# Moving the second pair of heads of the second batch behind the third feed-forward step

## The chip, the cores and the metric

The kernel runs on one core of one Trainium2 chip. The metric is the device time of one execution in microseconds; of the kernel before, three runs gave 924.9, 925.16 and 926.29 us, a median of 925.16 us. The engines are TensorE (PE in the profile, with PEld for its weight loads), VectorE (DVE), ScalarE (ACT), GpSimd (POOL) and SyncE (SP), which issues all data transfers here.

## The reference

Two parts follow each other. The first is attention over 8 batches of 8 heads, 576 tokens, 64 values a head; heads 0 to 3 see a window of the last 32 keys, heads 4 to 7 a window of 32 keys at a distance of 4. The second is a feed-forward layer over the 4608 tokens.

```
scores = scale * np.matmul(q, k.transpose(0, 1, 3, 2))
...
scores = np.where(masks[None, :, :, :], scores, -1000000000.0)
scores = scores - np.max(scores, axis=-1, keepdims=True)
attn = np.exp(scores)
attn = attn / (np.sum(attn, axis=-1, keepdims=True) + 1e-09)
return np.matmul(attn, v).astype(np.float32)
...
h = x @ w_in
g = np.where(pos, h, np.where(neg, 0.0, (h + beta) ** 2 / (4.0 * beta)))
return (g @ w_out).astype(np.float32)
```

w_in is 512 x 2048, w_out 2048 x 512. x is the attention's output with the heads of a token side by side.

## The kernel before, in words

Tokens are cut into 9 tiles of 512, the hidden dimension into 16 blocks of 128. A step is one tile and one block, so there are 144 steps; the first 16 are those of tile 0. Layer 1 of a step (L398) makes 12 products of 128 x 128 by 128 x 512 into one PSUM bank named h: each operand is held as a rounded part and a remainder, and three of the four cross terms are taken. Then DVE clips (L412), ACT squares (L415), DVE takes the maximum back into the bank (L417), ACT rounds it to gh (L418) and DVE makes the remainder gl (L421). Layer 2 (L434) runs two steps behind and adds 12 products into four banks named acc. There are two banks h, so layer 1 of step s waits for gl of step s-2.

Attention runs beside it. For heads 8 to 15 (the second batch) it goes in pairs (n, n+1), and each pair has five parts on TensorE: scores of four of six query tiles (L202), scores of the other two, transposes of n, transposes of n+1 (L325), and values (L360). DVE reduces each score tile with its mask (L176), softmax follows on POOL, ACT and DVE (L250, L284 to L286, L291 to L293), the transposes are copied out of PSUM by ACT and DVE (L328), and the values are copied out as a rounded part xh (ACT, L344) and a remainder xl (DVE, L345), in up to three pieces where a head's tokens cross a tile's border. Scores, transposes and values of these pairs share two PSUM banks (tag "att"): whatever comes next in one of them waits until the last reader of what stood there is done.

The weights arrive as 64-bit floats. For each of the 32 blocks ACT makes two passes over the words (L116, L120), DVE joins them (L121), ACT rounds (L126), POOL makes the remainder (L127). These blocks are prepared during the first 16 steps: from step 1 on, each step brings the layer-2 block of its own number and the layer-1 block three further on, behind the rounding of two steps earlier (L603 to L607). A buffer m, three deep, links L116 to the L127 of three blocks earlier.

The order on TensorE and on SP is that of the code (manual schedule). On DVE, ACT and POOL the compiler's scheduler fixes the order when the program is built, by its own estimate of times and by the priorities in the code; on the chip each of them then works in that order. A table (L479) gives the places of the pairs' parts: place 2s is between layer 1 of step s and layer 2 of step s-2, place 2s+1 is behind that layer 2. In the numbers of a tile's name, t10 is the transposes of head 10, o8 the values of heads 8 and 9, s12 the scores of head 12. At step 2 TensorE makes constant products that nothing reads (L610), after which layer 1 of step 2 follows.

Of the kernel before, what the change touches and what calls it, by code (L numbers as in the profile page):

```python
# [30 lines left out]
B, H, S, D = 8, 8, 576, 64  # L31
# [14 lines left out]
def body(ctx, tc, q, k, q2, k2, v, mask, eye, w_in, w_out, out):  # L46
# [23 lines left out]
    def load_pair(n):  # L70

        if 0 < n < H:
            qr, kr = borrow(f"qr{n}")[:, :S], borrow(f"kr{n}")[:, :KPAD]
        else:
            tags = ("qs", "kk") if n % 4 else ("qr", "kr")
            qr = pool.tile([128, S], F32, tag=tags[0], name=f"qr{n}")
            kr = pool.tile([128, KPAD + 32], F32, tag=tags[1], name=f"kr{n}")[:, :KPAD]
        nc.sync.dma_start(out=qr, in_=q[n // 2])
        nc.sync.dma_start(out=kr, in_=k[n // 2])
        for j in range(2):  # L80
            r = slice(64 * j, 64 * j + 64)
            heads[n + j] = dict(qs=qr[r], ks=kr[r])

    def load(n):
        qr = pool.tile([128, S], F32, tag="qr", name=f"qr{n}")
        kr = pool.tile([128, KPAD + 32], F32, tag="kr", name=f"kr{n}")[:, :KPAD]
        nc.sync.dma_start(out=qr, in_=q2[n - native])
        nc.sync.dma_start(out=kr, in_=k2[n - native])
        heads[n] = dict(qr=qr, kr=kr)
# [39 lines left out]
    def split(n):  # L129
        hd = heads[n]  # L130
        qs = pool.tile([128, S], F32R, tag="qs", name=f"qs{n}")
        kk = pool.tile([128, 2, KPAD], F32R, tag="kk", name=f"kk{n}")
        nc.scalar.copy(out=qs, in_=hd["qr"])
        nc.scalar.copy(out=kk[:, 0], in_=hd["kr"])  # L134
        nc.vector.tensor_tensor(
            out=qs[64:128], in0=hd["qr"][64:128], in1=qs[64:128].bitcast(F32), op=ALU.subtract
        )
        nc.gpsimd.tensor_tensor(out=kk[:, 1], in0=hd["kr"], in1=kk[:, 0].bitcast(F32), op=ALU.subtract)  # L138
        hd.update(qs=qs, ks=kk)
# [15 lines left out]
    def spin(times, bank):  # L155

        half = half_t.broadcast_to([128, 128])
        for _ in range(times):
            PE.matmul(out=bank[:, :128], lhsT=half, rhs=half, start=True, stop=True)  # L159
# [117 lines left out]
    def softmax(n):  # L277
        c, st = heads[n]["c"], heads[n]["st"]
        if n in (8, 9, 10, 12, 14):
            whole(n)  # L280
        else:
            for t in range(NQ):
                exp(n, t)
        nc.scalar.activation(out=st[:, 1], in_=st[:, 1], func=AF.Copy, bias=EPS)  # L284
        nc.vector.reciprocal(out=st[:, 2], in_=st[:, 1])  # L285
        nc.gpsimd.tensor_tensor(out=c, in0=c, in1=spread(st[:, 2]), op=ALU.mult)  # L286
# [43 lines left out]
    last = {}  # L330
    xt = {}

    def xtile(t):
        if t not in xt:
            xt[t] = (
                pool.tile([128, NC, TOK], F32R, tag="xh", name=f"xh{t}", bufs=3),
                pool.tile([128, NC, TOK], F32R, tag="xl", name=f"xl{t}", bufs=3),
            )
        return xt[t]
# [51 lines left out]
    def layer1(t, f, cs=range(NC), bank=("h", 2)):  # L391
        xh, xl = xtile(t)
        if cs[0] == 0 and (t, f) not in hps:
            hps[t, f] = ps.tile([128, TOK], F32, tag=bank[0], name=f"h{t}_{f}", bufs=bank[1])
        hp = hps[t, f]
        terms = [(w, x, c) for c in cs for w, x in ((0, xh), (1, xh), (0, xl))]
        for i, (w, x, c) in enumerate(terms):
            PE.matmul(  # L398
                out=hp,
                lhsT=wi[f][:, w, 128 * c : 128 * c + 128],  # L400
                rhs=x[:, c],
                start=c == 0 and i == 0,
                stop=c == NC - 1 and i == len(terms) - 1,
            )
        if cs[-1] < NC - 1:
            return
        del hps[t, f]
        y = pool.tile([128, TOK], F32, tag="y", name=f"y{t}_{f}")
        gh = pool.tile([128, TOK], F32R, tag="gh", name=f"gh{t}_{f}", bufs=2)
        gl = pool.tile([128, TOK], F32R, tag="gl", name=f"gl{t}_{f}", bufs=2)  # L410
        with tc.high_priority(offset=60):
            nc.vector.tensor_scalar(  # L412
                out=y, in0=hp, scalar1=-1.0, scalar2=1.0, op0=ALU.max, op1=ALU.min
            )
            nc.scalar.activation(out=y, in_=y, func=AF.Square, bias=half_t, scale=0.5)  # L415

            activated = nc.vector.tensor_tensor(out=hp, in0=hp, in1=y, op=ALU.max)  # L417
            copied = nc.scalar.copy(out=gh, in_=hp)  # L418
            if t == 0:
                last["g", f] = copied, activated  # L420
            nc.vector.tensor_tensor(out=gl, in0=hp, in1=gh.bitcast(F32), op=ALU.subtract)  # L421
        gs[t, f] = gh, gl

    acc = {}
# [28 lines left out]
    def place(u, *ops):  # L453
        slots.setdefault(u, []).extend(ops)

    def after_pair(n):
        softmax(n)
        softmax(n + 1)
        if n + 4 < native:
            load_pair(n + 4)  # L460
        elif n + 4 == native:
            load(native)
        else:
            split(native)
            load(native + 1)
# [10 lines left out]
        if n + 2 < native:  # L476
            load_values(n + 2)

    for n, at in ((8, (5, 6, 7)), (10, (1, 2, 8, 9, 10)), (12, (11, 12, 16, 17, 18)), (14, (19, 20, 24, 26, 30))):  # L479
        if n > H:  # L480
            place(at[0], lambda n=n: scores_pair(n, 0, 4))
            place(at[1], lambda n=n: (scores_pair(n, 4, NQ), after_pair(n)))
        turns = (n, n + 1) if n < 14 else (n + 1, n)
        for u, m in zip(at[-3:-1], turns):
            place(u, lambda m=m: transpose_pe(m))
        place(at[-1], lambda n=n: values_native(n))
# [66 lines left out]
    with tc.manual_schedule(engines={mybir.EngineType.PE, mybir.EngineType.SP}):  # L553
        pair(0)
        pair(2)
        pair(4)
        pair(6)
        hps[0, 0] = ps.tile([128, TOK], F32, tag="h", name="h0_0", bufs=2)
        early_transposes(0)
        load_values(8)  # L560
        fetch(1, w_out, "wo")
        fetch(4, w_in, "wi")
        load_pair(10)
        fetch(2, w_out, "wo")
        fetch(5, w_in, "wi")
        fetch(3, w_out, "wo")
        for f in range(6, 9):
            fetch(f, w_in, "wi")
            fetch(f - 2, w_out, "wo")
        early_values(0)  # L570
        early_transposes(2)
        early_values(2)
        first = marks()
        spin(10, hps[0, 0])
        early_transposes(4)
        spin(3, hps[0, 0])
        early_transposes(6)
        behind(first, ("wi", 0), ("wi", 1))
        early_values(4)
        second = marks()  # L580
        layer1(0, 0, range(2))
        early_values(6)
        third = marks()
        behind(second, ("wi", 2))
        layer1(0, 1, range(2))
        scores_pair(H, 0, 4)
        scores_pair(H, 4, NQ)
        for f in range(9, 14):
            fetch(f, w_in, "wi")
            fetch(f - 2, w_out, "wo")  # L590
        with tc.issue_after(third[0].ins), tc.issue_after(third[1].ins):
            after_pair(H)
        behind(third, ("wo", 0), ("wi", 3))
        l2 = 0
        steps = [(t, f) for t in range(NT) for f in range(NF)]
        lag = 2
        for s in range(len(steps) + lag):
            if s == 3:
                for f, src, name in ((12, w_out, "wo"), (13, w_out, "wo"), (14, w_in, "wi")):
                    fetch(f, src, name)  # L600
                for f, src, name in ((14, w_out, "wo"), (15, w_in, "wi"), (15, w_out, "wo")):
                    fetch(f, src, name)
            if 0 < s < NF:  # L603
                todo = [("wo", s)]
                if s + 3 < NF:
                    todo.append(("wi", s + 3))
                behind(last["g", max(s - 2, 0)], *todo)  # L607
            if s == 2:
                acc[0] = ps.tile([128, DM], F32, tag="acc0", name="acc0_0")
                spin(14, acc[0])  # L610
            if s < 2:
                layer1(*steps[s], range(2, NC))
            elif s < len(steps):
                layer1(*steps[s])
            run(2 * s)
            while l2 <= s - lag and l2 < len(steps):
                layer2(*steps[l2])
                l2 += 1
            run(2 * s + 1)
        assert not slots  # L620
# [63 lines left out]
```

## Time and profile before

| | us |
|---|---|
| median of three runs | 925.16 |
| the profiled execution | 924.59 |
| its span, first to last instruction | 922.8 |
| TensorE busy | 905.5 (98%) |
| DVE busy | 671.4 (73%) |
| ACT busy | 494.1 (54%) |
| POOL busy | 240.6 (26%) |
| mean granted TensorE clock | 0.998 |

The profile lists what each engine did in one execution. In a timeline a row is a start, a duration, engine, line and operation, output and inputs; in square brackets stands how long the engine was idle before it and what it was waiting for. Records of one engine overlap a little at their ends, so the distance between two starts is what an instruction takes up. A stretch row gives the busy time of an engine and the granted clock, where 1.00 is 2.4 GHz and 0.50 is 1.2 GHz. All times are microseconds from the start of the span unless marked ns.

### The profile page before, as it was taken

What the parts mean: (1) busy time and instruction counts of PE and PEld (TensorE: products, weight loads), DVE (VectorE), ACT (ScalarE), POOL (GpSimd) and SP (SyncE); (2) the same over time, 40 slices, a digit from 0 to 9 for tenths busy, and PEclk for the clock granted to TensorE, in tenths of its full rate; (3) what the DMA queues carried; (4) which work ended last, traced back from release to release, by engine and by line L of the source; (5) the groups of instructions that cost most, each with busy time, mean ns of one, the idle gap of its engine ahead of it and who ended that gap; (6) DMA issues with size and microseconds to landing.
All of it is one profiled execution on the core that took longest, in us unless ns stands there. A gap on an engine that the chain in (4) does not pass through costs nothing.

```text
span 922.8 us, 14430 instructions
## 1 busy us (share of the span) xinstructions
PE 905.5 (98%) x4886; PEld 743.0 (81%) x4886; DVE 671.4 (73%) x1966; ACT 494.1 (54%) x1352; POOL 240.6 (26%) x155
## 2 busy tenths in 40 slices
PE   7899999999999999999999999999999999999997
PEld 6677788888888888888888888888888888888886
DVE  6787778878888888788887888888888643334333
ACT  6798875555555556555555565555556322222222
POOL 4575453222222222222222222223222000000000
PEclk9999999999999999999999999999999999999999
DMA  9981013221232223112322223222321010001001
GB/s 352 407 309 46 1 27 105 82 64 55 66 116 71 70 71 112 48 61 64 116 71 71 70 64 104 63 71 71 116 71 44 1 46 1 1 1 47 0 1 47
DMA packets 31018, 73.87 MB, mean 80 GB/s; under 512 B 3520, under 2 KB 3808, under 8 KB 30944
## 3 DMA queue, kind: packets, MB, share of 16 engines
q1 hardware_dynamic: 30944, 72.94, 24.2%
q8 instruction: 39, 0.64, 0.3%
q14 instruction: 35, 0.29, 0.1%
HBM read 63.49 MB, written 9.44 MB: 79 GB/s over the span
## 4 chain that ended last, share of the span: by engine, by line
PE 89%; DMA 3%; POOL 2%; issue 2%; ACT 1%; DVE 1%; POOLq 0%; DVEq 0%; SPq 0%
PE acc L434 41%; PE h L398 40%; PE s L225 4%; PE o L360 3%; DMA wi_raw<-w_in 3%; ACT c L250 1%; POOL wi L127 1%; POOL wo L127 1%; POOL c L286 1%; PE s L159 0%; DVE c L293 0%; DVE c L176 0%; PE s L202 0%; PE t L325 0%; DMA out<-out 0%
## 5 line engine op out<-in xcount | busy, mean ns | idle before, releaser
L434 PE MATMUL acc<-wo,gh 128*128 128x512 f32 x1152 | 382.8, 393 | 0.0
L398 PE MATMUL h<-xh,wi 128*128 128x512 f32 x1152 | 356.9, 391 | 1.2 <-DVE gl L421 1.2
L434 PEld LDWEIGHTS acc<-wo,gh 128*128 128x128 f32 x1152 | 216.5, 188 | 47.2
L398 PEld LDWEIGHTS h<-xh,wi 128*128 128x128 f32 x1152 | 209.1, 188 | 39.4 <-DVE gl L421 1.4
L434 PE MATMUL acc<-wo,gl 128*128 128x512 f32 x576 | 225.1, 391 | 0.0
L398 PE MATMUL h<-xl,wi 128*128 128x512 f32 x576 | 224.2, 389 | 0.0
L138 POOL TENSOR_TENSOR kk<-kr,kk 128x608 fp32r<-128x608 f32 x48 | 94.8, 1974 | 413.1 <-ACT kk L134 413.1
L250 ACT ACTIVATE c<-c 96x128 f32<-96x128 f32 x330 | 129.0, 393 | 118.0 <-DVE c L176 118.0
L415 ACT ACTIVATE y<-y,consts 128x512 f32<-128x512 f32 x144 | 104.2, 724 | 117.6 <-DVE y L412 117.4
L418 ACT CAST gh<-h 128x512 fp32r<-128x512 f32 x144 | 84.4, 586 | 123.7 <-PE acc L434 119.9
L412 DVE TENSOR_SCALAR y<-h 128x512 f32<-128x512 f32 x144 | 99.2, 689 | 56.3 <-PE h L398 55.9
L417 DVE TENSOR_TENSOR h<-h,y 128x512 f32<-128x512 f32 x144 | 100.5, 698 | 49.6 <-ACT y L415 48.4
L421 DVE TENSOR_TENSOR gl<-h,gh 128x512 fp32r<-128x512 f32 x144 | 98.8, 686 | 40.9 <-ACT gh L418 40.8
L398 PEld LDWEIGHTS h<-xl,wi 128*128 128x128 f32 x576 | 108.2, 188 | 23.2
L434 PEld LDWEIGHTS acc<-wo,gl 128*128 128x128 f32 x576 | 108.2, 188 | 19.6
L301 DVE STREAM_TRANSPOSE pt<-c 32x192 f32<-32x192 f32 x288 | 106.0, 368 | 6.5 <-POOL c L286 3.1
L244 DVE TENSOR_TENSOR c<-s,msk 96x256 f32<-96x256 f32 (+1 forms) x168 | 61.4, 377 | 35.9 <-PE s L225 34.9
L286 POOL TENSOR_TENSOR c<-c 96x768 f32<-96x768 f32 x56 | 83.4, 1491 | 14.4 <-DVE c L285 14.4
L176 DVE CUSTOM_DVE_ANT_0 c<-s,c 96x128 f32<-96x128 f32 x288 | 70.6, 280 | 1.0
L250 ACT ACTIVATION_READ_ACCUMULATOR c<-c 96x1 f32 x330 | 62.2, 189 | 0.0
L344 ACT CAST xh<-o 128x288 fp32r<-128x288 f32 (+8 forms) x112 | 38.5, 383 | 38.4 <-PE o L360 24.1
L225 PEld LDWEIGHTS s<-kk,qs 128*96 128x96 f32 x288 | 46.3, 161 | 15.6
(57 smaller groups left out, 642.9 us busy)
## 6 DMA issues: line engine op xcount, KB each, us to landing
kr<-k_in SPq DMA_DIRECT2D x56, 304.0 KB, 3.3
qr<-q_in SPq DMA_DIRECT2D x56, 288.0 KB, 2.8
vt<-v_in SPq DMA_DIRECT2D x32, 384.0 KB, 3.9
out<-out SPq DMA_DIRECT2D x36, 256.0 KB, 3.1
wi_raw<-w_in SPq DMA_DIRECT2D x16, 512.0 KB, 9.2
wo_raw<-w_in SPq DMA_DIRECT2D x16, 512.0 KB, 9.6
msk<-mask_in SPq DMA_DIRECT2D x1, 144.0 KB, 3.6
ident<-eye_in SPq DMA_DIRECT2D x1, 36.0 KB, 4.3
```

The costliest lines, as they stand in the source:

```text
L138: nc.gpsimd.tensor_tensor(out=kk[:, 1], in0=hd["kr"], in1=kk[:, 0].bitcast(F32), op=ALU.subtract)
L225: PE.matmul(out=sv[:, t - t0], lhsT=hd["qs"][:, t * QT : (t + 1) * QT], rhs=hd["ks"][:, :, t * QT : t * QT + 128], start=True, stop=True,)
L250: last["act"] = nc.scalar.activation(out=c[:, t], in_=c[:, t], func=AF.Exp, bias=st[:, 0, t : t + 1], scale=-1.0, accum_out=st[:, 1, t : t ...
L286: nc.gpsimd.tensor_tensor(out=c, in0=c, in1=spread(st[:, 2]), op=ALU.mult)
L301: nc.vector.transpose(out=pt[r : r + 32, :, 32 * g : 32 * g + 32], in_=c[32 * g : 32 * g + 32, :, r : r + 32],)
L398: PE.matmul(out=hp, lhsT=wi[f][:, w, 128 * c : 128 * c + 128], rhs=x[:, c], start=c == 0 and i == 0, stop=c == NC - 1 and i == len(terms) - 1,
L412: nc.vector.tensor_scalar(out=y, in0=hp, scalar1=-1.0, scalar2=1.0, op0=ALU.max, op1=ALU.min)
L415: nc.scalar.activation(out=y, in_=y, func=AF.Square, bias=half_t, scale=0.5)
L417: activated = nc.vector.tensor_tensor(out=hp, in0=hp, in1=y, op=ALU.max)
L418: copied = nc.scalar.copy(out=gh, in_=hp)
L421: nc.vector.tensor_tensor(out=gl, in0=hp, in1=gh.bitcast(F32), op=ALU.subtract)
L434: PE.matmul(out=acc[m], lhsT=g[:, r], rhs=wo[f][:, w], start=f == 0 and i == 0, stop=f == NF - 1 and i == len(terms) - 1,)
```

## The change

The first scores of heads 10 and 11 move from place 1 to place 4, the second from place 2 to place 5, the transposes of heads 8 to 11 and the values of heads 8 and 10 one place later each. The softmax of heads 8 and 9 is now issued behind the rounding of step 0 instead of behind the last values of the first batch. The constant products at step 2 are 8, not 14. The pairs 12 and 14 keep their places.

```diff
-    for n, at in ((8, (5, 6, 7)), (10, (1, 2, 8, 9, 10)), (12, (11, 12, 16, 17, 18)), (14, (19, 20, 24, 26, 30))):
+    for n, at in ((8, (6, 7, 8)), (10, (4, 5, 9, 10, 11)), (12, (11, 12, 16, 17, 18)), (14, (19, 20, 24, 26, 30))):
...
-        with tc.issue_after(third[0].ins), tc.issue_after(third[1].ins):
-            after_pair(H)
...
-                spin(14, acc[0])
+                spin(8, acc[0])
             if s < 2:
                 layer1(*steps[s], range(2, NC))
+                if s == 0:
+                    with tc.issue_after(last["g", 0][0].ins):
+                        after_pair(H)
```

On TensorE, at places 10 and 11, the first scores of heads 12 and 13 (s12, s13) stood behind layer 2 of step 3. Before:

```order
L434 MATMUL acc0_3_787<-wo3_817,gh0_3_841 128x512
L434 MATMUL acc0_3_787<-wo3_817,gl0_3_842 128x512
L434 MATMUL acc0_3_787<-wo3_817,gh0_3_841 128x512
L202 MATMUL s12_0_1031<-kr12_618,qr12_617 96x128
L202 MATMUL s13_0_1033<-kr12_618,qr12_617 96x128
```

Now, in the same place:

```order
L360 MATMUL o10_1_1011<-pt1_68,vt10_921 64x96
L360 MATMUL o10_1_1011<-pt0_67,vt10_921 64x96
L360 MATMUL o10_1_1011<-pt1_68,vt10_921 64x96
L202 MATMUL s12_0_1025<-kr12_646,qr12_645 96x128
L202 MATMUL s13_0_1027<-kr12_646,qr12_645 96x128
```

The values of heads 10 and 11 (o10), which stood ahead of that layer 2, now stand directly ahead of the scores; both use the two shared banks.

On ACT, around the copies of those values out of PSUM (xh1 and xh2 from o10) and the work of step 5 (y0_5, gh0_5). Before:

```order
L344 CAST xh1_380<-o10_0_996 128x288
L126 CAST wi9_1061<-wi_m9_1057 128x512
L344 CAST xh1_380<-o10_1_1005 128x160
L415 ACTIVATE y0_5_988<-y0_5_988,consts_66 128x512
L344 CAST xh2_888<-o10_1_1005 128x128
L418 CAST gh0_5_989<-h0_5_975 128x512
L116 ACTIVATE wo_m7_1126<-wo_raw7_587 128x512
L120 ACTIVATE wo_raw7_587<-wo_raw7_587 128x512
```

Now:

```order
L415 ACTIVATE y0_5_972<-y0_5_972,consts_66 128x512
L418 CAST gh0_5_973<-h0_5_959 128x512
L116 ACTIVATE wo_m7_1120<-wo_raw7_587 128x512
L120 ACTIVATE wo_raw7_587<-wo_raw7_587 128x512
L116 ACTIVATE wi_m10_1127<-wi_raw10_589 128x512
L120 ACTIVATE wi_raw10_589<-wi_raw10_589 128x512
L344 CAST xh1_380<-o10_0_1002 128x288
L344 CAST xh1_380<-o10_1_1011 128x160
L126 CAST wo7_1124<-wo_m7_1120 128x512
L126 CAST wi10_1131<-wi_m10_1127 128x512
L344 CAST xh2_917<-o10_1_1011 128x128
```

The copies stood ahead of the rounding of step 5; now the rounding and four passes over the weight blocks wo7 and wi10 stand ahead of them, and two more roundings ahead of the last copy.

On ACT, around the copies of the values of heads 8 and 9 (o8) and the copy of the transposes of head 10 (t10). Before:

```order
L344 CAST xh1_380<-o8_0_870 128x288
L116 ACTIVATE wo_m4_894<-wo_raw4_350 128x512
L418 CAST gh0_3_841<-h0_3_827 128x512
L120 ACTIVATE wo_raw5_354<-wo_raw5_354 128x512
L344 CAST xh1_380<-o8_1_879 128x160
L120 ACTIVATE wi_raw8_356<-wi_raw8_356 128x512
L116 ACTIVATE wi_m7_901<-wi_raw7_352 128x512
L126 CAST wo4_898<-wo_m4_894 128x512
L116 ACTIVATE wo_m5_961<-wo_raw5_354 128x512
L344 CAST xh2_888<-o8_1_879 128x128
L328 COPY pt0_67<-t10_0_929 128x384
```

Now:

```order
L344 CAST xh1_380<-o8_0_899 128x288
L126 CAST wo4_868<-wo_m4_864 128x512
L344 CAST xh1_380<-o8_1_908 128x160
L126 CAST wi7_875<-wi_m7_871 128x512
L116 ACTIVATE wo_m5_945<-wo_raw5_354 128x512
L418 CAST gh0_4_892<-h0_4_878 128x512
L120 ACTIVATE wo_raw6_358<-wo_raw6_358 128x512
L120 ACTIVATE wi_raw9_585<-wi_raw9_585 128x512
L344 CAST xh2_917<-o8_1_908 128x128
L328 COPY pt0_67<-t10_0_935 128x384
```

The copies of o8 stood among the work of step 3 and now stand among that of step 4, the last of them behind that step's rounding.

## Rows read from the trace of the kernel before

**Rows 1.** The page's line of busy times, and two rows of the list of who waited for whom on TensorE (us in total, times, longest us).

```profile
PE 905.5 (98%) x4886; PEld 743.0 (81%) x4886; DVE 671.4 (73%) x1966; ACT 494.1 (54%) x1352; POOL 240.6 (26%) x155
...
PE t L325 <- ACT pt L328: 1.2, 1, 1.2
PE h L398 <- DVE gl L421: 1.2, 1, 1.2
```

**Rows 2.** Stretches of TensorE: from:to, length, busy us (instructions), granted clock, busy share of the transfer engines, GB/s.

```profile
46.00:47.00 1.00, 1.00 (x7) 0.50 1.00 401
...
49.00:50.00 1.00, 1.00 (x11) 0.96 1.02 404
...
98.00:922.00 824.00, 819.92 (x4235) 1.00 0.19 58
```

**Rows 3.** Timeline of TensorE at steps 1 to 3.

```profile
44.62 0.46 PE L202 MATMUL s<-kr,qr 64*96 64x128 f32 x2 [1.62 <-DVE c L176]
45.46 1.01 PE L202 MATMUL s<-kr,qr 64*96 64x128 f32 x6 [0.39 <-DVE c L176]
46.40 4.65 PE L159 MATMUL acc<-consts 128*128 128x128 f32 x28
50.81 0.71 PE L398 MATMUL h<-xh,wi 128*128 128x512 f32 x2
...
58.19 0.73 PE L398 MATMUL h<-xh,wi 128*128 128x512 f32 x2 [1.18 <-DVE gl L421]
```

**Rows 4.** Timeline of TensorE at steps 4 to 8.

```profile
66.28 0.73 PE L398 MATMUL h<-xh,wi 128*128 128x512 f32 x2
...
70.86 0.39 PE L325 MATMUL t<-ident,c 96*128 96x96 f32 x2 [1.23 <-ACT pt L328]
...
74.31 0.70 PE L398 MATMUL h<-xh,wi 128*128 128x512 f32 x2
...
78.56 0.50 PE L434 MATMUL acc<-wo,gh 128*128 128x512 f32 x1
...
81.51 1.12 PE L202 MATMUL s<-kr,qr 64*96 64x128 f32 x16
82.56 0.74 PE L398 MATMUL h<-xh,wi 128*128 128x512 f32 x2
...
97.64 0.71 PE L325 MATMUL t<-ident,c 96*128 96x96 f32 x6 [0.31 <-POOL c L286]
```

**Rows 5.** Timeline of DVE: the clip and the remainder of step 0.

```profile
43.05 0.68 DVE L412 TENSOR_SCALAR y<-h 128x512 f32<-128x512 f32 x1
...
48.23 0.68 DVE L421 TENSOR_TENSOR gl<-h,gh 128x512 fp32r<-128x512 f32 x1
```

**Rows 6.** Groups of instructions between 40 and 100 us: line, engine, operation, shapes, count, then busy us and mean ns of one, then the idle time before them.

```profile
L121 DVE SCALAR_TENSOR_TENSOR wi_m<-wi_m,wi_raw 128x512 uint32<-128x512 uint32 x10 | 9.9, 992 | 1.0 <-ACT wi_m L116 1.0
L121 DVE SCALAR_TENSOR_TENSOR wo_m<-wo_m,wo_raw 128x512 uint32<-128x512 uint32 x9 | 9.9, 1101 | 1.7 <-ACT wo_raw L120 1.5
...
L176 DVE CUSTOM_DVE_ANT_0 c<-s,msk 96x128 f32<-96x128 f32 x34 | 7.6, 280 | 0.0
L415 ACT ACTIVATE y<-y,consts 128x512 f32<-128x512 f32 x9 | 6.5, 727 | 0.8 <-DVE y L412 0.8
L417 DVE TENSOR_TENSOR h<-h,y 128x512 f32<-128x512 f32 x9 | 6.2, 689 | 1.0 <-ACT y L415 1.0
L126 ACT CAST wi<-wi_m 128x512 fp32r<-128x512 f32 x10 | 6.2, 620 | 3.3 <-DVE wi_m L121 3.3
...
L250 ACT ACTIVATE c<-c 96x128 f32<-96x128 f32 x12 | 4.7, 402 | 0.0
...
L418 ACT CAST gh<-h 128x512 fp32r<-128x512 f32 x8 | 4.6, 576 | 2.3 <-PE acc L434 1.8 <-DVE c L285 0.5
...
L293 DVE TENSOR_REDUCE c<-c 96x6 f32<-96x768 f32 x4 | 3.8, 940 | 0.5 <-ACT c L292 0.5
...
L292 ACT ACTIVATE c<-c 96x768 f32<-96x768 f32 x4 | 3.3, 830 | 0.0
```

**Rows 7.** Timeline of ACT: the rounding of step 5 and the four weight passes behind it; the last row shows where the passes end.

```profile
81.62 0.58 ACT L418 CAST gh<-h 128x512 fp32r<-128x512 f32 x1 [1.30 <-PE acc L434]
82.10 0.67 ACT L116 ACTIVATE wo_m<-wo_raw 128x512 f32<-128x512 f32 x1
82.67 0.68 ACT L120 ACTIVATE wo_raw<-wo_raw 128x512 uint32<-128x512 uint8 x1
...
84.34 0.42 ACT L250 ACTIVATE c<-c 96x128 f32<-96x128 f32 x1
```

**Rows 8.** Timelines of ACT and DVE: first and last copy of the values of head 10 out of PSUM, and the last copy of those of head 8 (72.14).

```profile
78.36 0.40 ACT L344 CAST xh<-o 128x288 fp32r<-128x288 f32 x1
...
72.14 0.28 DVE L345 TENSOR_TENSOR xl<-o,xh 128x128 fp32r<-128x128 f32 x1
...
80.81 0.28 DVE L345 TENSOR_TENSOR xl<-o,xh 128x128 fp32r<-128x128 f32 x1
```

**Rows 9.** Timeline of SP's queue: the load of the queries of head 14, and the loads of the values of heads 10 and 12.

```profile
46.65 0.33 SPq L78 DMA_DIRECT2D qr<-q_in  x1
...
62.62 4.09 SPq L96 DMA_DIRECT2D vt<-v_in  x2
```

## Prediction

> **What bounds the kernel now.** I read the page's busy times first: TensorE is busy 905.5 of 922.8 us [rows 1]. So the time is TensorE's work plus its idle stretches. The stretches say where those are: from 98 us to 922 us TensorE is busy 819.92 of 824 us at full clock [rows 2], and what is missing lies at the very end. The change touches nothing there: behind place 12 the order on every engine is as it was. So whatever it gains or loses is decided before 98 us, and from there on the rest only shifts. I therefore compare, block by block, when layer 1 of a step starts now and when it will start.
>
> The list of waits and the timeline of TensorE give the losses there. At step 1 the second scores of heads 10 and 11 wait 1.62 and 0.39 us for the score reductions, after which the clock falls: 0.50 at 46 to 47 us, back to full at 49 (0.96 in the next stretch) [rows 2, 3]. Then the 14 constant products, begun at 46.40, take 4.65 us, so that layer 1 of step 2 starts at 50.81, though gl of step 0, which it needs, ends at 48.23 + 0.68 = 48.91 [rows 3, 5]. Layer 1 of step 3 waits 1.18 us for gl of step 1, the transposes of head 10 wait 1.23 us, those of head 12 wait 0.31 us [rows 1, 3, 4].
>
> **The change, gate by gate.** An engine works in its built order, so I follow the new orders with the durations of [rows 6]; records overlap by about 0.1 us (a weight pass of 0.67 is followed by the next after 82.67 - 82.10 = 0.57 [rows 7]), so a pass takes up 0.56, a square 0.62, a rounding gh 0.46, a weight rounding 0.52, an exponential 0.39 with its readout (two rows of one head), the long exponential 0.74, a DVE clip, maximum or remainder 0.60, a score reduction 0.21, a row sum 0.86.
>
> Step 2. With the second pair's scores gone, DVE goes from the clip of step 0 (43.05, unchanged [rows 5]) straight to square, maximum, rounding, remainder: 43.05 + 0.68 + 0.73 + 0.69 + 0.58 + 0.68, and some 0.1 of hand-overs, gives 46.5. The eight products, at a quarter of a microsecond each at full clock (4.65 us for 14, most of it at half clock, is an estimate's basis), are over by then: they wait only for one bank of head 8's scores, read by about 42.7. Step 2 starts at 46.5, not 50.81: 4.3 earlier. Six products fewer are inside this gain, not beside it.
>
> Step 3 needs gl of step 1. ACT goes on at 45.7: long exponential, seven passes, square of step 1: 45.7 + 0.74 + 3.92 + 0.62 = 51.0. DVE: maximum 51.7; now the eight reductions of the moved scores, which stand ahead of everything else here: 53.4; row sum 54.3; clip 54.9; remainder 55.6. Step 3 starts at 55.6, not 58.19: 2.6 earlier. So part of the gain is given back.
>
> Step 4 needs gl of step 2. DVE from 55.6: four reductions, a weight join that waits for ACT's pass until 57.1, maximum, join, clip, join, copy, remainder. A join (L121) takes 0.99 to 1.10 on the mean [rows 6], about 0.97 net: 57.1 + 0.97 + 0.1 + 0.6 + 0.97 + 0.6 + 0.97 + 0.26 + 0.68 = 62.3. TensorE itself is ready at 62.2. Step 4 starts at 62.4, not 66.28: 3.9 earlier.
>
> Step 5. The transposes of head 10 now come 2.85 us (one layer 2) behind the values of head 8, and their second half goes into the bank that the last copy of those values sets free. Before, they reused the other bank, and had to wait only for ACT's copy, 1.23 us [rows 4]; the last copy of head 8's values ran at 72.14, well behind the transposes [rows 8]. The new ACT order from gh of step 1 (53.9) to that copy holds 14 passes, 5 weight roundings, 6 exponentials, 3 gh, 3 squares, a long exponential and copies of 1.5 in all: 7.84 + 2.60 + 2.34 + 1.38 + 1.86 + 0.74 + 1.5 = 18.3, without a gap. That gives 72.2, with the copy and DVE's part 72.7. Step 5 starts at 72.95, not 74.31: only 1.4 earlier. TensorE stands idle for some 3 us here.
>
> Step 6. This is the place that decides. The values of head 10 are now directly followed by the scores of heads 12 and 13 in the same two banks. Before, layer 2 of step 3 lay between (78.56 to 81.51 [rows 4]), and the copies, 78.36 to 80.81 + 0.28 = 81.09 [rows 8], were done behind it. Now nothing covers them, and ACT's copies stand behind step 5's square and rounding, which stand behind three weight joins on DVE. From 72.95: copy of the transposes, join, rounding, join, pass, join: clip of step 5 at 77.6 (TensorE had finished that block at 75.8). From the clip on: join's rounding and a copy on ACT 0.93, square, maximum, gh: 80.5; four passes 2.25 (82.10 to 84.34 in [rows 7]): 82.75; first copy, xl behind a weight join: 83.9; two weight roundings, last copy, xl: 84.8. Then 0.95 for the rest of the scores: step 6 starts at 85.75, not 82.56: 3.2 later. TensorE was ready for the scores at 80.3, so it idles 4.5 us.
>
> Bounds of that: the clip can't be before 75.9 (layer 1 of step 5), which gives step 6 at 84.0, +1.5. Joins of about 0.3 more each, for POOL's work beside them, give 86.8, +4.2. I take +3.2, by the mean join.
>
> The clock. Before, it fell after idle stretches of 1.62 and 0.39 us with 0.4 us of work between [rows 3], and 3.2 us at half rate cost 1.6. A stretch of 4.5 us should do no less; that is +1.6, bounds 0 (it stays up) and 2.3 (half rate for the whole of scores, layer 1 and more: 4.6 us, an estimate). A fall in the idle stretch ahead of step 5 costs nothing more, since the clip of step 5 waits for DVE until 77.6 anyway.
>
> The Trainium skill, page "TensorE: Matmul & The Clock Gate", section "A second HAM failure mode: psum-queue depth-cycling", says that short idle times between groups of matmuls, made by cycling through PSUM banks, are enough to bring the clock down again and again. Here the trace agrees once and disagrees three times: it fell at 46 us, not in the idle 1.18, 1.23 and 0.31 us later. By the rule the smaller new waits ahead of steps 2 to 4 would each cost 1.6 too; the orders on ACT and DVE would hide most of that.
>
> Behind step 6: the wait of 0.31 us for head 12 goes (its softmax has slack then), -0.3. The loads on SP move as well: head 14's queries go into the buffer of head 10's, so the load issued at 46.65 waits for the moved scores, to about 54, and the values of head 10 behind it in the queue go from 62.62 [rows 9] to about 63.5; they are wanted at 79, so 15 us hide it. Without that cover the values would wait for the load, and step 6 with them.
>
> **Sum.** +3.2 + 1.6 - 0.3 = +4.5 on the profiled execution's own 924.59: 929.1. The median of the three runs is 925.16, 0.6 above it, so by the median 929.7. I say 929.3.
>
> **Rivals.** (a) Faster: the copies are not late. If head 10's values are copied out as fast as before (2.5 us from their end), and step 5's wait is small, the gain of 3.9 at step 4 reaches the end of these values: 78.56 - 3.9 = 74.7, + 2.5 + 1.05 gives step 6 at 78.2, 4.3 earlier; with the 0.3, and a clock that may fall once, 921. For it: the 2.5 us are a row; against it: the built order puts the copies behind gh and four passes. 0.13. (b) No change: the clip of step 5 comes right behind layer 1 and the clock stays up: 924.59 + 1.5 - 0.3 = 925.8. For it: some joins run beside an idle POOL. 0.13. (c) The late copies as forecast, but the clock stays up: 927.5, 0.12. (d) By the rule on short waits, one more fall that nothing hides: 930.9, 0.07. (e) That the change doesn't move the second pair's scores is excluded by the orders shown.
>
> **How the numbers follow.** The forecast has 0.55, at 929.3, its own range 925.8 to 931.4 (the bounds of step 6 and of the clock: +1.2 to +6.2, with the 0.6). Two runs of this kernel differ by less than 0.2%, 1.85 us, so that bounds "same". Faster 0.13 from (a), same 0.13 from (b), slower 0.74 from the rest. The range for 8 in 10 leaves out (a) and a small piece above: 924.0 to 931.8.
>
> **What would show it.** Right: layer 1 of step 2 at about 46.5 and of step 4 at 62 to 63; an idle stretch of 2 to 3 us in the transposes of head 10, put down to xl (L345); 4 to 5 us of idle time ahead of the scores of heads 12 and 13, again to xl; a granted clock of 0.50 at about 85 to 88 us. Wrong: these scores starting within 2.5 us of the values' end; step 6 starting before 82.56; gl of step 2 later than 64, which would mean that the joins, not ACT's list, set the pace.

## The result, and the profile after

The changed kernel takes 932.88 us (median of four), the kernel before beside it 925.03: a ratio of 1.0088, 95% interval 1.0075 to 1.0100. So it is slower, as forecast, but by 7.85 us and not by some 4.5; 932.88 is above the range of 924.0 to 931.8.

The profiled execution (934.16, span 932.4) is the slowest of the four. Its page and its list of waits on TensorE (us in total, times, longest):

```profile
PE 906.7 (97%) x4874; PEld 743.0 (80%) x4874; DVE 672.5 (72%) x1966; ACT 494.7 (53%) x1352; POOL 241.3 (26%) x155
...
PE s L202 <- DVE xl L345: 4.4, 2, 4.2
PE h L398 <- DVE gl L421: 3.2, 2, 1.9
...
PE t L325 <- DVE xl L345: 1.9, 1, 1.9
PE t L325 <- DVE pt L328: 1.7, 1, 1.7
```

Beside [rows 1], TensorE's work grew by 1.2 us, although it has twelve matmuls fewer: part of it ran at half clock. The wait of the transposes for ACT's copy is gone and those for the reductions are smaller. Those for gl grew from 1.2 to 3.2 us, a wait of 1.7 for a copy of transposes is new, and xl is now waited for at two places, once for 4.2 us. Both places stand in the timeline of TensorE, which answers to [rows 4]:

```profile
74.35 0.36 PE L325 MATMUL t<-ident,c 96*128 96x96 f32 x2 [1.86 <-DVE xl L345]
74.48 0.71 PE L398 MATMUL h<-xh,wi 128*128 128x512 f32 x2
...
81.43 1.21 PE L360 MATMUL o<-pt,vt 128*64 128x96 f32 x24 [0.67 <-ACT pt L328]
86.83 0.74 PE L202 MATMUL s<-kr,qr 64*96 64x128 f32 x2 [4.19 <-DVE xl L345]
87.78 1.99 PE L202 MATMUL s<-kr,qr 64*96 64x128 f32 x14 [0.21 <-DVE xl L345]
89.70 1.22 PE L398 MATMUL h<-xh,wi 128*128 128x512 f32 x2
```

The stretches of TensorE there (from:to, length, busy us (instructions), granted clock, share of the transfer engines, GB/s), as in [rows 2]:

```profile
84.00:86.00 2.00, 0.00 (x0) 0.54 0.02 4
86.00:88.00 2.00, 0.96 (x4) 0.50 0.00 0
...
92.00:94.00 2.00, 2.00 (x6) 0.50 0.03 8
94.00:96.00 2.00, 2.00 (x13) 0.90 0.00 0
```

The clock fell to 1.2 GHz in the idle stretch and came back only behind 94 us: the first scores and nearly all of layer 1 of step 6 ran at half rate. The last two things to read are ACT at the copies, and DVE and POOL at the joins:

```profile
82.82 0.59 ACT L418 CAST gh<-h 128x512 fp32r<-128x512 f32 x1 [0.82 <-DVE h L417]
83.30 0.67 ACT L116 ACTIVATE wo_m<-wo_raw 128x512 f32<-128x512 f32 x1
...
84.95 0.67 ACT L120 ACTIVATE wi_raw<-wi_raw 128x512 uint32<-128x512 uint8 x1
85.50 0.61 ACT L344 CAST xh<-o 128x288 fp32r<-128x288 f32 x2
...
61.22 2.59 DVE L121 SCALAR_TENSOR_TENSOR wi_m<-wi_m,wi_raw 128x512 uint32<-128x512 uint32 x1
63.73 0.34 DVE L328 COPY pt<-t 128x192 f32<-128x192 f32 x1
64.00 0.68 DVE L421 TENSOR_TENSOR gl<-h,gh 128x512 fp32r<-128x512 f32 x1
...
75.82 1.57 DVE L121 SCALAR_TENSOR_TENSOR wo_m<-wo_m,wo_raw 128x512 uint32<-128x512 uint32 x1
78.64 1.70 DVE L121 SCALAR_TENSOR_TENSOR wi_m<-wi_m,wi_raw 128x512 uint32<-128x512 uint32 x1 [1.25 <-ACT wi_m L116]
80.27 0.68 DVE L412 TENSOR_SCALAR y<-h 128x512 f32<-128x512 f32 x1
...
84.60 0.69 DVE L121 SCALAR_TENSOR_TENSOR wo_m<-wo_m,wo_raw 128x512 uint32<-128x512 uint32 x1 [0.47 <-ACT wo_raw L120]
...
60.11 1.92 POOL L286 TENSOR_TENSOR c<-c 96x768 f32<-96x768 f32 x1
61.99 1.27 POOL L127 TENSOR_TENSOR wi<-wi_m,wi 128x512 fp32r<-128x512 f32 x1
...
75.29 1.55 POOL L127 TENSOR_TENSOR wo<-wo_m,wo 128x512 fp32r<-128x512 f32 x1 [0.76 <-ACT wo L126]
76.80 1.74 POOL L127 TENSOR_TENSOR wi<-wi_m,wi 128x512 fp32r<-128x512 f32 x1
78.51 1.29 POOL L127 TENSOR_TENSOR wo<-wo_m,wo 128x512 fp32r<-128x512 f32 x1
```

On ACT the four passes run between gh and the copies, as the built order said. On DVE a join takes 0.69 while POOL is idle (84.60), and a join that meets a running POOL instruction ends 0.54 to 0.57 us behind that instruction, or behind the next one: 61.22 + 2.59 = 63.81 behind 61.99 + 1.27 = 63.26; 75.82 + 1.57 = 77.39 behind 75.29 + 1.55 = 76.84; 80.34 behind 79.80. The first of these joins waited for two POOL instructions in a row, as the one at 61.99 started while it waited. In the second case the join came in between, and the next POOL instruction is the longer one: 1.74.

The starts of layer 1, from the timelines. Profiled executions differ by up to some 1 us ahead of step 1, so the last row counts from there.

| us | step 1 | 2 | 3 | 4 | 5 | first s12 | 6 | 7 | 9 |
|---|---|---|---|---|---|---|---|---|---|
| before | 38.70 | 50.81 | 58.19 | 66.28 | 74.31 | 81.51 | 82.56 | 89.00 | 101.40 |
| after | 39.16 | 47.20 | 56.22 | 64.73 | 74.48 | 86.83 | 89.70 | 98.28 | 110.18 |
| after less before, from step 1 | 0 | -4.07 | -2.43 | -2.01 | -0.29 | +4.86 | +6.68 | +8.82 | +8.32 |

Four microseconds are gained at step 2, nothing of them is left at step 5, and the loss arises between step 5 and step 7. Behind step 9 the difference stays; 0.8 us of the 9.57 between the two profiled executions lie behind the last matmul, in the output's transfers.

### The profile page after: what moved, and what is told of

Same layout as the page of the kernel before. It is cut to its first block, busy times and chain, and to the rows that moved or that the text cites. A ratio compares the mean times of both kernels' runs of the same rounds, so it can differ in the third digit from the quotient of the medians.

```text
span 932.4 us, 14404 instructions
## 1 busy us (share of the span) xinstructions
PE 906.7 (97%) x4874; PEld 743.0 (80%) x4874; DVE 672.5 (72%) x1966; ACT 494.7 (53%) x1352; POOL 241.3 (26%) x155
## 4 chain that ended last, share of the span: by engine, by line
PE 91%; DMA 5%; ACT 2%; DVE 1%; issue 0%; SPq 0%; DVEq 0%; ACTq 0%
PE acc L434 42%; PE h L398 41%; DMA wi_raw<-w_in 4%; PE s L225 4%; PE o L360 3%; DMA kr<-k_in 1%; DVE wi_m L121 1%; PE s L202 0%; ACT wi_m L116 0%; ACT wo_raw L120 0%; ACT wi_raw L120 0%; ACT wo L126 0%; PE t L325 0%; ACT wo_m L116 0%; DMA out<-out 0%
```

## The experiments

Theory A: the loss is made where the values of head 10 now stand directly ahead of the scores of heads 12 and 13 in the same two banks: a wait for late copies, and a clock that falls in it. Theory B: it is made by the moved softmax and by joins held up beside POOL in steps 3 to 5. The shares below overlap and don't add up to the loss. All kernels ran in five rounds beside the kernel before, whose medians were 925.55 (first four kernels), 925.32 (next four), 925.25 (next three) and 925.14.

**One number of the table alone**, in the kernel before.

```diff
-(10, (1, 2, 8, 9, 10))
+(10, (1, 2, 8, 9, 11))
```

> The kernel before with one number of the table changed: the values of heads 10 and 11 at place 11 instead of 10, so directly ahead of the scores of heads 12 and 13. Everything else of the change is left out. Theory A (the loss is this neighbourhood of values and scores in two shared banks, plus the clock that falls in the wait): the built order puts the copies behind gh of step 5 and four passes, as in the changed kernel; layer 1 of step 6 starts near 85.5 us instead of 82.56, after a wait of 2.5 to 4 us put down to xl, and then runs at half clock, 2 to 4 us more: 930 to 932. Theory B (the loss comes from the moved softmax and the joins beside it in steps 3 to 5): none of that is here, 924.5 to 926. If A is right but the clock stays up: 927.5 to 928.5.

Measured 931.97, ratio 1.0063 (1.0050 to 1.0075): theory A. TensorE's timeline, one of its stretches, and DVE and POOL ahead of the clip of step 5:

```profile
80.96 1.21 PE L360 MATMUL o<-pt,vt 128*64 128x96 f32 x24
85.84 0.74 PE L202 MATMUL s<-kr,qr 64*96 64x128 f32 x2 [3.67 <-DVE xl L345]
...
88.00:90.00 2.00, 2.00 (x9) 0.50 0.00 0
...
77.55 0.69 DVE L121 SCALAR_TENSOR_TENSOR wo_m<-wo_m,wo_raw 128x512 uint32<-128x512 uint32 x1 [0.51 <-ACT wo_raw L120]
78.98 0.69 DVE L121 SCALAR_TENSOR_TENSOR wi_m<-wi_m,wi_raw 128x512 uint32<-128x512 uint32 x1 [0.74 <-ACT wi_m L116]
79.58 0.68 DVE L412 TENSOR_SCALAR y<-h 128x512 f32<-128x512 f32 x1
...
79.53 1.29 POOL L127 TENSOR_TENSOR wo<-wo_m,wo 128x512 fp32r<-128x512 f32 x1 [1.94 <-ACT wo L126]
```

Nearly the same wait and the same half clock, with nothing else of the change in the code: by the medians 6.4 us, where the whole change costs 7.85. The five executions lie in two groups, 929.87 and 930.13, and 931.97 to 932.64.

The last rows part the two theories' shares. Here POOL is idle when the joins ahead of the clip of step 5 come; they take 0.69 each, and the clip runs 79.58 - 75.31 = 4.27 us behind the start of step 5. In the changed kernel, with joins of 1.57 and 1.70, it is 80.27 - 74.48 = 5.79. Counted from step 1, the first scores come 3.42 us later than before, in the changed kernel 4.86. So the chain with joins beside POOL is some 1.5 us longer; the two kernels differ in ACT's order there as well, which may have a part in it. The rest of the delay needs only the neighbourhood.

**Scores of heads 10 and 11 back at places 1 and 2, all else changed.**

```diff
-(10, (4, 5, 9, 10, 11))
+(10, (1, 2, 9, 10, 11))
```

> The changed kernel with the scores of heads 10 and 11 back at places 1 and 2, so that only transposes and values lie a place later and the softmax of heads 8 and 9 behind step 0. Theory A (the loss comes from values 10 directly ahead of the scores of heads 12 and 13, whatever the scores of heads 10 and 11 do): a wait of 2.5 to 4.5 us for xl ahead of the former, half clock behind it, 930 to 933.5. Rival (the loss comes from the reductions of the moved scores among steps 2 and 3): 925 to 927.

933.82, 1.0095 (1.0081 to 1.0109), just above the range of theory A. The wait for xl is there again (2.9 us) and the clock falls behind it, although the scores of heads 10 and 11 stand where they stood. But this kernel has losses of its own: waits of 3.5 and 3.0 us for gl and POOL appear ahead of steps 3 and 4, and the granted clock falls behind both (0.61 at 58 to 60 us, 0.50 at 70 to 72). So it shows that the wait for xl doesn't need the moved scores; what their move costs or brings can't be read from its time.

**Transposes and values back at the old places, scores and softmax moved.**

```diff
-(8, (6, 7, 8)), (10, (4, 5, 9, 10, 11))
+(8, (5, 6, 7)), (10, (4, 5, 8, 9, 10))
```

> The changed kernel with the transposes and values of heads 8 to 11 back at their old places (5, 6, 7 and 8, 9, 10); the scores of heads 10 and 11 stay at 4 and 5, the softmax behind step 0 and the 8 products stay. Theory A: layer 2 of step 3 lies between values 10 and the scores of heads 12 and 13 again, no wait above 1.5 us there, no half clock behind 84 us, and the gain of the early steps (step 2 by 3.6 us, step 4 by 1.5) reaches the end at least in part: 921.5 to 923.5. Theory B (moved softmax, joins beside POOL): step 5 and step 6 are late all the same, 928 or more. Theory C (whatever is gained early is taken back by DVE and ACT before step 6): 924.5 to 925.5.

932.71, 1.0075 (1.0063 to 1.0088). The number lies in theory B's range, not in A's, and steps 5 and 6 are late, as B says. The collision ahead of heads 12 and 13 is gone, and another wait has taken its place:

```profile
57.85 1.22 PE L325 MATMUL t<-ident,c 96*128 96x96 f32 x6 [4.02 <-POOL c L286]
```

With the softmax of heads 8 and 9 issued behind step 0, POOL is not done with it when place 5 comes, and the clock stands at 0.50 from 56 to 66 us. So here the moved softmax does cost. The changed kernel has the transposes of head 8 a place later, and there they don't wait (59.09). This kernel can't speak for theory A, as the later softmax needs the later transposes.

**Scores of heads 12 and 13 a place later, so that layer 1 of step 6 covers the copies.**

```diff
-(12, (11, 12, 16, 17, 18))
+(12, (12, 13, 16, 17, 18))
```

> The changed kernel with the scores of heads 12 and 13 one place later (12 and 13 instead of 11 and 12), so that layer 1 of step 6 covers the copies of values 10. Theory A: step 6 starts right behind values 10, at 82.3 to 82.8 us; the scores behind it wait 0.5 to 1.8 us for xl, since the copies end at 86.3 and 87.3; the clock stays up or falls for a short time: 925.5 to 928. Theory B: 931 or more, since steps 3 to 5 are untouched.

929.70, 1.0042 (1.0028 to 1.0056): 3.2 less than the changed kernel, where 5 to 7 were expected. Step 6 starts at 82.25 and the clock stays at 1.00, as A says; the scores still wait 1.25 and 0.66 us for xl, and the transposes of head 12 now wait 1.00 for POOL.

**Constant products in the idle stretch.** They go into the bank h that step 6 will use and that is free there.

```diff
+    def warm(n):
+        if n == 12:
+            hps[0, 6] = ps.tile([128, TOK], F32, tag="h", name="h0_6", bufs=2)
+            spin(18, hps[0, 6])
...
-            place(at[0], lambda n=n: scores_pair(n, 0, 4))
+            place(at[0], lambda n=n: (warm(n), scores_pair(n, 0, 4)))
```

> The changed kernel with 18 constant products more, ahead of the scores of heads 12 and 13, into the free bank h of step 6: 18 times 0.23 us at full clock fill the idle stretch of 4.19 us. The wait for the copies stays, only TensorE is not idle in it. It parts the clock term from the wait: if the half clock from 84 to 94 us is the consequence of the idle stretch, the granted clock stays at 1.00 there and 3.5 to 4.5 us come back: 928.4 to 929.5. If the clock term is only the 1.6 us forecast: 931.3. If the fall has another cause: 932.5 to 933.5, with 0.50 still in the stretches behind 86 us.

930.42, 1.0055 (1.0042 to 1.0067): 2.46 less than the changed kernel, between the two expectations. TensorE's timeline and a stretch:

```profile
81.92 4.28 PE L159 MATMUL h<-consts 128*128 128x128 f32 x36
86.17 0.46 PE L202 MATMUL s<-kr,qr 64*96 64x128 f32 x2
87.12 1.08 PE L202 MATMUL s<-kr,qr 64*96 64x128 f32 x14 [0.49 <-DVE xl L345]
...
88.00:90.00 2.00, 2.00 (x11) 1.00 0.04 8
```

The wait is as long, the clock stays at 1.00. From the first scores to step 7 it now takes 94.56 - 86.17 = 8.39 us, in the changed kernel 98.28 - 86.83 = 11.45: the clock costs 3.06 in the profiled execution and 2.46 by the medians.

**ACT's copies ahead of the four passes.** TensorE's order is untouched; the two weight blocks of step 7 are issued behind the copies.

```diff
-                behind(last["g", max(s - 2, 0)], *todo)
+                if s == 7:
+                    behind(marks(), *todo)
+                else:
+                    behind(last["g", max(s - 2, 0)], *todo)
```

> The changed kernel, where the weight blocks of step 7 (wo7, wi10) are issued behind the copies of values 10 instead of behind the rounding of step 5, so that ACT makes the copies ahead of the four passes and DVE ahead of two joins. TensorE's order is untouched. Theory A (ACT's order makes the copies late, and the clock follows from the wait): copies at 83.4 to 84 instead of 85.5 to 87.3, the scores of heads 12 and 13 start at 84.3 to 84.8 instead of 86.83, the idle stretch is 2 instead of 4.2 us, the clock falls for a short time or not at all: 926 to 928.5. If the wait shrinks and the clock still falls for as long: 930.5. If the order on ACT doesn't matter: 932.5 to 933.5.

930.97, 1.0071 (1.0058 to 1.0084), near the 930.5 that was expected if the clock still fell. The place is right: the first copy runs at 83.22, the scores start at 84.46 after 1.91 us instead of 4.19. The clock seems to decide the rest, and differently from one execution to the next: the five took 933.13, 932.99, 930.97, 930.85 and 930.20 at mean clocks of 0.996, 0.996, 0.997, 0.998 and 0.998. The profiled one is the slowest, and there it fell:

```profile
84.46 0.74 PE L202 MATMUL s<-kr,qr 64*96 64x128 f32 x2 [1.91 <-DVE xl L345]
...
84.00:86.00 2.00, 1.33 (x8) 0.52 0.00 0
...
90.00:92.00 2.00, 2.00 (x9) 0.77 0.00 0
```

**Both: copies first, and 8 constant products in what idle time is left** (with the function of the 18 products).

```diff
+            spin(8, hps[0, 6])
```

> The kernel of the copies-first experiment (930.97) with 8 constant products in what is left of the idle stretch ahead of the scores of heads 12 and 13 (1.9 us). The wait stays, the idle stretch goes. If the half clock from 84 to 91.5 us there comes from these 1.9 us of idleness, the scores and layer 1 of step 6 run at full clock, 2.9 us less (14 scores in 1.08 instead of 1.99, layer 1 in 2.85 instead of 4.6 us): 927.5 to 928.5. If it comes from the run of short stretches before (1.08, 1.86, 1.34, 1.66, 1.85 us): no gain, 930.5 or more.

930.52, 1.0059 (1.0046 to 1.0072): by the time alone no gain, and not the 927.5 to 928.5 expected from a clock that stays up. Yet the profiled execution keeps the clock at 1.00 in every stretch from 42 to 116 us, and starts step 7 at 92.74 where the copies alone started it at 95.42. That gain of 2.68 fits the profiled execution of the copies alone (933.13), not their median, since in three of five executions the clock seems to have stayed up anyway. Without idle wait and without half clock there remain 5.3 us over the kernel before. Counted from step 1, step 7 starts 3.45 us later than before: the products stand for 2 us of wait, the second bank comes 0.49 late, the values wait 0.67 for ACT, and the transposes of head 11 (0.44), which before were made ahead of step 5, lie behind it. Behind step 7 the transposes of head 12 wait 0.90 for POOL, before 0.31. The rest is not put down to a cause here.

**Joins without POOL's subtraction.** POOL fills the remainders of three weight blocks with zeros, so that this part of the weights is left out of the products.

```diff
+        if (name, f) in (("wo", 5), ("wi", 8), ("wo", 6)):
+            nc.gpsimd.memset(w[f][:, 1].bitcast(F32), 0.0)
+        else:
             nc.gpsimd.tensor_tensor(out=w[f][:, 1], in0=mf, in1=w[f][:, 0].bitcast(F32), op=ALU.subtract)
```

> The changed kernel, where POOL fills the remainders of three weight blocks (wo5, wi8, wo6) with zeros instead of subtracting, so that this part of the weights' precision is left out; POOL's instructions beside the joins of wo6 and wi9 become short and read nothing. One pass on ACT (the first of wi9) comes two places earlier by it. Theory: these two joins took 1.57 and 1.70 us because they stood beside POOL's subtractions; without them 0.7 each, so the clip of step 5 comes at 77.3 to 78.3 (as forecast, 77.6) instead of 80.27, layer 1 of step 6 at 85 to 87 instead of 89.70, and the time falls by 2 to 5 us: 928 to 931. Rival (the joins are long by themselves, or the clip is held by ACT's chain alone): clip at 79.5 or later, 932 or more.

930.23, 1.0061 (1.0048 to 1.0074), 2.65 less than the changed kernel. DVE and POOL in its profile (lines behind L126 are numbered 2 or 3 higher):

```profile
76.01 0.69 DVE L121 SCALAR_TENSOR_TENSOR wo_m<-wo_m,wo_raw 128x512 uint32<-128x512 uint32 x1
76.62 0.68 DVE L121 SCALAR_TENSOR_TENSOR wi_m<-wi_m,wi_raw 128x512 uint32<-128x512 uint32 x1
79.26 0.69 DVE L415 TENSOR_SCALAR y<-h 128x512 f32<-128x512 f32 x1 [1.95 <-PE h L401]
...
76.11 0.53 POOL L128 MEMSET wi<- 128x512 f32 x1 [0.95 <-DVE wi_m L121]
76.76 0.53 POOL L128 MEMSET wo<- 128x512 f32 x1
```

The joins take 0.69 and 0.68 with a fill beside them, and are over at 77.30. The clip waits for TensorE alone, and comes at 79.26 only because in this execution the clock fell in the wait ahead of step 5:

```profile
74.51 0.55 PE L328 MATMUL t<-ident,c 96*128 96x96 f32 x2 [1.86 <-DVE xl L348]
...
76.00:78.00 2.00, 2.00 (x6) 0.53 0.01 4
```

That wait, 1.86 us long in both kernels, left the clock at 1.00 in the changed kernel's profile. The profiled execution is again the slowest (932.40; three of five took 929.42 to 930.23); in it the clock fell a second time behind a wait of 2.86 us for xl ahead of the scores of heads 12 and 13 (0.53 at 88 to 90 us). One pass on ACT also comes earlier in this kernel, so the 2.65 us are not the joins' alone.

**The front of the kernel before.** Four kernels ask whether time can be had ahead of step 5: 8 constant products instead of 14; 7 ahead of the second scores of heads 10 and 11 and 11 behind them; the layer-1 block of weights a step later; that block and the layer-2 block a step later.

```diff
-                spin(14, acc[0])
+                spin(8, acc[0])
...
-                acc[0] = ps.tile([128, DM], F32, tag="acc0", name="acc0_0")
-                spin(14, acc[0])
+                spin(11, acc[0])
...
+                if s == 1:
+                    acc[0] = ps.tile([128, DM], F32, tag="acc0", name="acc0_0")
+                    spin(7, acc[0])
...
-                if s + 3 < NF:
-                    todo.append(("wi", s + 3))
+                if 1 < s and s + 2 < NF:
+                    todo.append(("wi", s + 2))
...
-                todo = [("wo", s)]
+                todo = [("wo", s - 1)] if s > 1 else []
...
+                if s == NF - 1:
+                    todo.append(("wo", s))
```

> The kernel before with 8 constant products instead of 14 at step 2; nothing else of the change (two neighbouring instructions on ACT change places). At half clock a product takes 0.43 us, so they end near 49.9 instead of 50.81, still behind gl of step 0 (48.91). If step 3 follows step 2 (its gl stands on DVE behind the copy of transposes that TensorE makes behind layer 2 of step 0): 0.6 to 1 us earlier, 924.5 to 925. If DVE and ACT set step 3: no change, 925.3 to 925.8. A share of the loss in the changed kernel would need 926.5 or more.

> The kernel before with 7 constant products in the idle stretch ahead of the second scores of heads 10 and 11 (43.0 to 44.6) and 11 instead of 14 at step 2; DVE then makes gl of step 0 ahead of the last four score reductions. If the clock stays at 1.00 from 44 to 50 us, the products end near 48.7 and step 2 starts at 48.2 to 49 instead of 50.81. Theory (this front is a plain cost of the kernel before, and can be had without the change): 1 to 2 us less, 923.5 to 924.5. If DVE and ACT take it back before step 5, as they took back the gain of the changed kernel: 925 to 925.8. If the clock falls all the same: 925.5 or more.

> The kernel before, where each step from step 2 on brings the layer-1 block two steps ahead instead of three, so that ACT and DVE have one block less (1.7 us of ACT, 0.7 to 1.7 of DVE) to make ahead of step 5. Theory (DVE and ACT, not TensorE's order, set when steps 3 to 6 start, so that taking work from them gains and moving TensorE's work does not): step 5 starts 0.5 to 1.7 us earlier than 74.31, 923.5 to 925. If the late block is wanted before it is there, or the order merely turns elsewhere: 925.3 or more.

> The kernel before, where each step brings the layer-1 block two steps ahead instead of three and the layer-2 block of the step before instead of its own, so that ACT and DVE have two weight blocks less to make ahead of step 5. The late layer-1 block alone gave 924.73 beside 925.25 (ratio 0.9995, not to be told from no change). Theory (ACT and DVE set the start of steps 3 to 6): 0.5 to 1 us less again, 923.5 to 924.5. If the blocks come too late for layer 2, or the front is not the bound any more: 925 or more.

Measured: 925.51, 1.0003 (0.9994 to 1.0012); 927.32, 1.0023 (1.0013 to 1.0033); 924.73, 0.9995 (0.9986 to 1.0004); 927.29, 1.0027 (1.0016 to 1.0038). Counted from step 1, step 3 starts 1.05, 1.05, 0.07 and 1.31 us earlier than before, step 5 later by 1.01, 2.58, earlier by 0.35, and later by 1.51. Three times a gain turns into a new wait, of 1.73, 3.34 and 3.04 us, at the values of head 8 or the transposes of head 10, and each time the clock falls in it or behind it (0.50 at 68 to 70, 68 to 70 and 72 to 74 us). So part of what these three lose by step 5 is half clock. With the later layer-1 block alone the clock stays at 1.00 from 60 to 80 us. With the 7 products the clock does stay at 1.00 from 42 to 50 us; the later wait is made by DVE:

```profile
63.26 3.79 DVE L121 SCALAR_TENSOR_TENSOR wi_m<-wi_m,wi_raw 128x512 uint32<-128x512 uint32 x1
66.97 0.34 DVE L328 COPY pt<-t 128x192 f32<-128x192 f32 x1
...
58.82 5.24 POOL L286 TENSOR_TENSOR c<-c 96x768 f32<-96x768 f32 x3
64.03 1.25 POOL L127 TENSOR_TENSOR wi<-wi_m,wi 128x512 fp32r<-128x512 f32 x1
65.25 1.25 POOL L127 TENSOR_TENSOR wo<-wo_m,wo 128x512 fp32r<-128x512 f32 x1
```

This join came while POOL worked without a pause and was held for all of it, and the copy that TensorE wants stands behind the join. The 8 products alone and the later layer-1 block can't be told from no change; the other two kernels are slower, the one with the 7 products above everything that was expected of it for a clock that stays up. No kernel here is shown to beat the kernel before.

## Why the prediction was wrong in size

**Right.** The direction, and the place: "This is the place that decides." Values 10 directly ahead of the scores of heads 12 and 13 cost 6.4 us in the kernel before, with nothing else moved. Counted from step 1, steps 2 and 3 came 4.07 and 2.43 earlier (forecast 4.3 and 2.6), and the chain from the clip of step 5 to the first scores took 86.83 - 80.27 = 6.56 (forecast 83.9 - 77.6 = 6.3). The slack behind step 7 brought 0.5 (forecast 0.3). Of the signs named, step 2 at 46.5 (47.20, or 46.74 with step 1 at 38.70), the wait of 4 to 5 us for xl and the half clock came; the wait for xl in the transposes of head 10 was 1.86, not 2 to 3. Rival (a) is refuted by the late copies, (b) and (c) by the clock. (d), one more fall, is not what happened either, though its 930.9 lies nearer: there was no second fall behind step 1, and the one that came cost more.

**The step that failed first: "A join (L121) takes 0.99 to 1.10 on the mean, about 0.97 net."** The mean of [rows 6] mixes joins of 0.68 with joins of up to 1.96. The three that stand on the chain took 2.59, 1.57 and 1.70: 5.86 instead of 2.91. Chiefly by the first of them step 4 gained 2.0 instead of 3.9; the prediction's own sign for this came, "gl of step 2 later than 64, which would mean that the joins, not ACT's list, set the pace": it ran from 64.00 to 64.68. Step 5 gained 0.3 instead of 1.4, and there the joins are only a part: ACT's last copy of head 8's values ran at 73.50, forecast 72.2, behind an idle 0.38 us for the late layer 2 of step 2, and xl came behind a join of 1.42. The two others held the clip of step 5: it came at 80.27 instead of 77.6, beyond the bound of "about 0.3 more each". From step 1, the first scores came 4.86 later, where 83.9 against 81.51 had been 2.4. Of these 2.5 us, 1.1 arose ahead of step 5, 1.1 between it and its clip, 0.3 behind the clip. The zeros, and the kernel with one number changed, show joins of 0.69 where POOL doesn't read beside them. The Trainium skill states this rule, on the page "SBUF — State Buffer", section "Who interferes with whom": a DVE instruction with two inputs in SBUF contends with a GpSimd instruction that reads SBUF, not with one that only writes it, and such contention is an exclusive lock. The rows agree: 1.57 and 1.70 us beside POOL's subtractions, 0.69 and 0.68 beside its fills.

**The second term: the clock, "+1.6, bounds 0 and 2.3".** It cost 2.46 by the medians, 3.06 in the profiled execution, above its bound: half rate lasted to behind 94 us, nearly to the end of layer 1 of step 6. The 1.6 came from another fall, at 46 us. The bound was mis-sized as well. In the kernel before, the second scores of heads 12 and 13 follow layer 1 of step 6:

```profile
85.54 0.68 PE L202 MATMUL s<-kr,qr 64*96 64x128 f32 x8
```

So the first scores and layer 1 take 85.54 - 81.51 = 4.03 us at full clock, and half rate for the whole of them costs some 4.0 by this estimate, not 2.3. (The lower end of the forecast's own range, 925.8, lacks the 0.6 that the upper end has; nothing hangs on it.)

In the profiled execution the sum is 4.86 for the first scores, 0.90 for the second bank (8.39 us from the first scores to step 7 with the products, 89.00 - 81.51 = 7.49 before), 3.06 for the clock, -0.50 behind step 7: 8.32, then 0.46 ahead of step 1 and 0.8 behind the last matmul: 9.57. Forecast were 3.2 for the first two, 1.6 and -0.3.

That the moved scores bring nothing by step 5 was half foreseen ("part of the gain is given back"). The front kernels point to why: work moved on TensorE doesn't shorten what DVE and ACT have to do ahead of step 5. That DVE and ACT alone set it is argued, not shown: of those four kernels one lightened their load and gained 0.35 us there, one that lightened it more lost by another order, and in three the clock fell as well.

## What to carry to other kernels

Before work is moved off a stalled engine, ask which engine the next two waits belong to; if they belong to the engines that feed it, the gain may be returned there, and the move may only create a new neighbour. Two uses of the same PSUM bank without other matmuls between them exposed, here, the whole queue of the engine that empties the bank. And price an instruction by its duration beside the work that will run beside it, not by the mean of its group.

## What the runs showed of the hardware

- DVE's join of two SBUF operands made no headway beside POOL's TENSOR_TENSOR instructions: 0.69 us with POOL idle, 3.79 at worst, its end 0.54 to 0.57 behind POOL's. Where POOL had its next instruction ready, the waiting join came in between in some cases (75.82) and had to wait for the next one too in others (61.22, and 63.26 with the 7 products); what decides this is open. POOL pays as well: a subtraction of 1.29 took 1.74 when a join ran first.
- The same idle stretch can bring the clock down or not: 1.86 us ahead of step 5 left it at 1.00 in the changed kernel and at 0.53 behind it with the zeros; with the copies first, the five executions lie in two groups some 2 us apart, at mean clocks of 0.996 and of 0.997 to 0.998. The Trainium skill's account of clocks brought down by short waits (page "TensorE: Matmul & The Clock Gate", section "A second HAM failure mode: psum-queue depth-cycling") holds here as something that may happen, not as something that does: the waits of 1.9 and 1.7 us for gl, xl and the copy of transposes in the changed kernel's profile left it at 1.00.
